# Turning f by DMA transfers in place of TensorE in a fused linear-attention and MLP kernel

## The chip, the core and the metric

The kernel runs on one core of a Trainium2 chip. The metric is device time in microseconds (us), the median of several executions. Times are compared only with runs of the kernel before on the same chip in the same rounds.

Engine names in the profile: PE is TensorE (matrix products and transposes), DVE is VectorE, ACT is ScalarE, POOL is GpSimd, SP is SyncE, which here only issues transfers. "SPq" and "POOLq" are the queues from which SP and GpSimd issue transfers.

## The reference, cut to what matters

```python
# B=4, H=8, S=768, D=48
f = 1 / (1 + exp(-f_logit))
for t in range(S):
    state = f[:, :, t, :, None] * state + einsum('bhd,bhe->bhde', k[:, :, t], v[:, :, t])
    y[:, :, t] = einsum('bhd,bhde->bhe', q[:, :, t], state)
x  = y as (B, S, 384)
xn = (x - mean) / sqrt(var + 1e-6) * g_ln
out = x + maximum(xn @ w_ch1, 0) @ w_ch2          # 384 -> 1536 -> 384
```

Everything is float32. The recurrence is computed in 12 units of 64 tokens, all four batches at once. The weights arrive as 8-byte words and are converted on the chip in the start part.

## The kernel before

The program is written as two lists of tokens, which fix the order of instructions on every engine. `START` holds the first three units with the conversion of the weights. `UNIT` is repeated for the MLP of units 3 to 11 (`m`) with the attention of later units (`n = m+1`, `o = m+2`, `p = m+3`) woven in. `m3` is one step of the MLP of unit 3, `a5.gates` a step of the attention of unit 5, `l6f` the load of unit 6's f.

```python
UNIT = """
m{m} m{m} m{m} a{n}.carried a{o}.after a{n}.scores a{n}.causal m{m} m{m} a{n}.values m{m} m{m}
m{m} m{m} a{n}.stats m{m} m{m} m{m} a{n}.norm m{m} m{m} m{m} s{m} a{n}.chunk
m{m} a{n}.turn m{m} a{o}.upto a{p}.gates a{o}.kx l{p}v a{o}.k a{n}.state m{m} m{m} m{m}
a{o}.kt y{n} m{m} a{o}.q l{p}q l{p}x a{o}.kept l{p}k m{m} l{z}f
"""
```

f comes with tokens in the partitions and is wanted with channels there. TensorE turns it, eight transposes of 128x128, and ScalarE takes the sigmoid out of PSUM. `fraw` is one buffer: the next load waits until it has been read.

```python
def across(src, g):
    pt = one_bank(f"tr{n}")
    for a in range(NP):
        nc.tensor.transpose(pt[:, a * P:(a + 1) * P],
                            src[:, g, 2 * a:2 * a + 2].rearrange("p h e -> p (h e)"), ident)
    return pt.rearrange("p (s t) -> p s t", t=T)

def do_gates():
    ...
    for g in range(G):
        pt = across(loaded[n, "f"], g)
        nc.scalar.activation(out=gv[:, segs, 1:E1], in_=pt, func=AF.Sigmoid)
```

The LayerNorm's `rstd` is made on GpSimd; xn on VectorE needs it. Behind xn in VectorE's order stands an add that is needed by ScalarE's relu, and the fifth of the six matmul steps of p1 reads what that relu writes:

```python
def do_stats():
    ...                                        # mean and variance on VectorE
    nc.gpsimd.tensor_scalar_add(out=rstd, in0=mv[:, :, 1], scalar1=EPS)
    nc.gpsimd.tensor_tensor(out=rstd, in0=rstd, in1=power, op=ALU.pow)

# by_blocks, the first layer:
    add((1, 2), product("bz", y[6], b[2, 2]))  # VectorE, behind xn in its order
    relu((1, 2))                               # ScalarE
# the second layer:
    nc.scalar.copy(out=p1, in_=product("p1", a11, b11))   # steps 5 and 6 read block (1, 2)
```

Of the kernel before, what the change touches and what calls it, by code (L numbers as in the profile page):

```python
# [8 lines left out]
FP32 = mybir.dt.float32  # L9
I32 = mybir.dt.int32  # L10
U32 = mybir.dt.uint32
AF = mybir.ActivationFunctionType
ALU = mybir.AluOpType
PSUM = bass.MemoryType.PSUM
# [288 lines left out]


START = """
l0k f l0q a0.gates l0x a0.after l0v f r a0.kx a0.upto l1f
d a0.kept a0.k d l1x d d a0.q l1k a0.carried d a0.scores
d a0.causal a0.values w d r a0.kt a0.stats f l1q d a1.gates
f l1v a0.chunk d w a0.norm a1.after a0.state a0.turn d a1.upto a1.kx
a1.k d f r w m0 a1.kept m0 a1.q f f r  # L310
w a1.carried a1.kt r f r l2k f a1.scores a1.causal f l2v
w l2f f a1.values r a1.chunk f a1.stats m0 m0 r w
a1.norm m0 a1.turn r w r w a1.state m0 m1 m1 m1
w m1 w a2.gates r m0 m1 m0 a2.after r l2x w
l2q w a2.kx a2.k a2.upto m1 m0 a2.q m0 m0 l3q l3k
a2.kept l3v m0 a2.carried a2.scores U m1 a2.causal a2.values m1 a2.stats a2.norm
m1 m1 U l3f a2.kt U m1 a2.turn m1 a3.gates T a2.chunk
m2 a3.after a2.state a3.kx l3x l4f m2 a3.k a3.upto a3.kept m2 a3.q
U m2 U l4q a3.carried a3.scores a3.kt U U a3.causal U l4x
a4.gates l4k a3.values T l4v U U a3.chunk m2 a3.stats a3.state t  # L320
l5v U a3.norm m2 s2 a4.after m2 l5f a3.turn m2 m2 a4.kx
a4.k a4.upto l5x l5k m2 U u m2 a4.q m2 y3 l5q
a5.gates a4.kt m2 l6f a4.kept
"""
UNIT = """
m{m} m{m} m{m} a{n}.carried a{o}.after a{n}.scores a{n}.causal m{m} m{m} a{n}.values m{m} m{m}
m{m} m{m} a{n}.stats m{m} m{m} m{m} a{n}.norm m{m} m{m} m{m} s{m} a{n}.chunk
m{m} a{n}.turn m{m} a{o}.upto a{p}.gates a{o}.kx l{p}v a{o}.k a{n}.state m{m} m{m} m{m}
a{o}.kt y{n} m{m} a{o}.q l{p}q l{p}x a{o}.kept l{p}k m{m} l{z}f
"""  # L330


# [1 line left out]
def kernel(  # L334
# [19 lines left out]
    nc = tc.nc  # L354
    B, H, S, D = q.shape
    P = 128
    T = 64
    G = B // 2
    NP = H // 2
    GA = G * NP  # L360
    NS = 2 * GA
    E1 = T + 1
# [4 lines left out]
    NU = S // T  # L367
# [2 lines left out]
    LEAST = 1e-12  # L370
    PLAIN = 2
    FIRST = 3
    PIECE = 768

    outer = ctx.enter_context(tc.tile_pool(name="outer", bufs=1))
# [9 lines left out]
    raws = fast.enter_context(tc.tile_pool(name="raws", bufs=2))  # L385
    work = fast.enter_context(tc.tile_pool(name="work", bufs=1))
    xs = fast.enter_context(tc.tile_pool(name="xs", bufs=3))
    ps2 = fast.enter_context(tc.tile_pool(name="ps2", bufs=2, space=PSUM))
    ps1 = fast.enter_context(tc.tile_pool(name="ps1", bufs=4, space=PSUM))

    changing = ExitStack()
    stage = changing.enter_context(tc.tile_pool(name="stage", bufs=2))

    def two_banks(name):
        return ps2.tile([P, 2, 512], FP32, tag="two", name=name)

    def one_bank(name):
        return ps1.tile([P, 512], FP32, tag="one", name=name)
# [11 lines left out]
    def load(n, name, engines=(nc.sync,)):  # L410
        if n >= NU:
            return
        if name == "x":

            loaded[n, name] = raws.tile([P, G, NP, D], FP32, tag="rawx", name=f"vx{n}")
            odd = v.rearrange("b (a r) s d -> b r s a d", r=2)
            for b in range(B):
                nc.sync.dma_start(out=loaded[n, name][(1 - b % 2) * T:(2 - b % 2) * T, b // 2],
                                  in_=odd[b, 1, n * T:(n + 1) * T])
            return  # L420
        if name == "v":
            vt = raws.tile([P, G, H, D], FP32, tag="rawv", name=f"v{n}")
            loaded[n, name] = vt
        else:
            loaded[n, name] = wide_heads[name]
        src = {"f": f_logit, "k": k, "q": q, "v": v}[name]
        for b in range(B):
            engines[b % len(engines)].dma_start(  # L428
                out=loaded[n, name][(b % 2) * T:(b % 2 + 1) * T, b // 2, :, 0:D],
                in_=src[b, :, n * T:(n + 1) * T, :].rearrange("h p d -> p h d"))  # L430

    load(0, "f", (nc.sync, nc.scalar))

# [161 lines left out]
    def attention(n):  # L595
# [7 lines left out]
        def new(name, shape, **kw):  # L603
            at[name] = work.tile(shape, FP32, tag=name, name=f"{name}{n}", **kw)
            return at[name]
# [6 lines that stand above are left out]
                                    src[:, g, 2 * a:2 * a + 2].rearrange("p h e -> p (h e)"),  # L612
                                    ident)
            return pt.rearrange("p (s t) -> p s t", t=T)
# [20 lines left out]
        def times(dst, pts, by):  # L635
            for g, pt in enumerate(pts):
                segs = slice(g * HS, (g + 1) * HS)
                nc.vector.tensor_tensor(out=dst[:, segs], in0=pt, in1=by[:, segs, 1:E1],  # L638
                                        op=ALU.mult)

        def do_gates():
            new("after", [P, NS, E1])
            new("upto", [P, NS, E1])
            new("total", [P, NS], bufs=2)
            for g in range(G):
                segs = slice(g * HS, (g + 1) * HS)
                pt = across(loaded[n, "f"], g)
                nc.scalar.activation(out=gv[:, segs, 1:E1], in_=pt, func=AF.Sigmoid)  # L648
                if n == 0:
                    scan_after(segs)  # L650
                    scan_upto(segs)
# [7 lines left out]
                scan_upto(slice(0, NS))  # L659

        def do_k_across():
            at["pk"] = [across(loaded[n, "k"], g) for g in range(G)]

        def do_k():
            times(new("kh", [P, NS, T]), at["pk"], at["after"])

        def do_q():
            times(new("qh", [P, NS, T]), [across(loaded[n, "q"], g) for g in range(G)],
                  at["upto"])
            nc.vector.tensor_tensor(out=least, in0=least, in1=at["total"], op=ALU.min)  # L670

        def do_kept():
# [6 lines left out]

        def do_carried():  # L680

            at["py"] = py = two_banks(f"py{n}")
            if not n:
                return
            qh, kept = at["qh"], at["kept"]
            for e in range(GA):
                for b in range(2):
                    for r in range(2):
                        nc.tensor.matmul(py[half(b), r, e * D:(e + 1) * D],  # L689
                                         lhsT=qh[head_rows(r), 2 * e + b],  # L690
                                         rhs=kept[head_rows(r), b, e], start=e == 0, stop=False,
                                         skip_group_check=True)
# [285 lines left out]




    running = {}

    def run(plan):
        for token in plan.split():
            kind, rest = token[0], token[1:]
            if kind == "a":
                n, stage = rest.split(".")
                if int(n) >= NU:
                    continue  # L990
                if "a" + n not in running:
                    running["a" + n] = attention(int(n))
                running["a" + n].pop(stage)()
            elif kind == "m":
                if token not in running:
                    running[token] = mlp(int(rest))
                next(running[token])
            elif kind == "l":
                load(int(rest[:-1]), rest[-1])
            elif kind == "s":  # L1000
                sums(int(rest))
            elif kind == "y":
                if FIRST <= int(rest) < NU:
                    sums_of_x(int(rest))
            else:
                {"r": read, "w": write, "f": fetch, "t": mix, "d": idle,
                 "T": lambda: mix(nc.gpsimd), "u": mix_step,
                 "U": lambda: mix_step(nc.gpsimd)}[token]()
# [2 lines left out]
    assert not (queue or fetched or opened)  # L1011
    for m in range(3, NU):
        run(UNIT.format(m=m, n=m + 1, o=m + 2, p=m + 3, z=m + 4))
        if m == NU - 2:
            worst = consts.tile([P, 1], FP32)
            nc.vector.tensor_reduce(out=worst, in_=least, axis=mybir.AxisListType.X, op=ALU.min)
            pw = one_bank("pw")
            nc.tensor.transpose(pw[0:1, 0:P], worst, ident)
            least_one = consts.tile([1, 1], FP32)
            nc.vector.tensor_reduce(out=least_one, in_=pw[0:1, 0:P], axis=mybir.AxisListType.X,  # L1020
                                    op=ALU.min)
            nc.vector.tensor_scalar(out=small, in0=least_one, scalar1=LEAST, scalar2=None,
                                    op0=ALU.is_lt)
# [37 lines left out]
```

## Time and profile before

The kernel before takes 476.49 us (475.71 to 476.61). Its profiled execution was a quicker one, of 472.8 us.

| | before |
|---|---|
| span of the profiled execution | 470.7 us |
| TensorE busy | 96% |
| GpSimd busy | 20% |
| first product of the first repeated unit (bw of m3) | 152.52 us |
| one repeated unit | 36.13 us |

Two more lines are used later. The first is from the page's groups (line, engine, operation, names, shapes, count, then total busy us, mean ns of one, and idle us ahead of the group). The second fence is the windows view of one unit: for each engine busy us and, in brackets, its instructions, then TensorE's granted clock, DMA share and GB/s.

```profile
L935 PE MATMUL pp<-w,h 128*128 128x192 f32 x240 | 42.9, 329 | 0.0
```

```profile
297.03:333.16 36.13, 36.13 (x500) 35.43 (x499) 26.95 (x48) 11.46 (x24) 3.64 (x6) 1.00 0.32 62
```

One instruction takes 329 ns; two of them, which overlap with their neighbours, make one step of a product. TensorE never waits ahead of this group. In the unit it is busy for 36.13 us of 36.13 at full clock, VectorE for 27, GpSimd for 3.6. So TensorE's work is the time, and GpSimd seems free.

### The profile page before, as it was taken

How to read it: one execution, taken by the hardware profiler on the slowest of the kernel's cores; microseconds unless marked ns; L12 is line 12 of the kernel's file. 1: busy time of each engine (PE TensorE's matmuls, PEld its weight loads, DVE VectorE, ACT ScalarE, POOL GpSimd, SP SyncE). 2: the span in 40 equal slices, each digit the busy share in tenths (PEclk: the TensorE clock that was granted, in tenths of full speed). 3: DMA queues.
4: the chain of work that ended last, by engine and by line, in shares of the span. 5: the costliest groups of instructions: out<-in, count | busy, mean ns of one | idle time of the engine just before them, and what ended most of it. 6: DMA issues, size and time to landing. Idle time of an engine off the chain costs nothing.

```text
span 470.7 us, 13070 instructions
## 1 busy us (share of the span) xinstructions
PE 452.5 (96%) x5655; PEld 420.3 (89%) x5655; DVE 332.3 (71%) x543; ACT 149.7 (32%) x298; POOL 93.9 (20%) x110
## 2 busy tenths in 40 slices
PE   5698999999999999999999999999999999999994
PEld 4487887668899999999999999999999999999994
DVE  6798978236698688578678678677768768666361
ACT  3256652013321341341251242243142241241320
POOL 3215534079222011011011011002002002002010
PEclk9989999999999999999999999999999999999998
DMA  9899980623463302512522522422422410100001
GB/s 167 163 215 239 262 218 2 135 45 65 81 117 78 76 3 55 99 35 52 96 43 52 101 37 50 87 54 43 92 54 42 78 36 9 29 1 18 17 10 33
DMA packets 125969, 36.32 MB, mean 77 GB/s; under 512 B 116432, under 2 KB 122064, under 8 KB 125904
## 3 DMA queue, kind: packets, MB, share of 16 engines
q1 hardware_dynamic: 124128, 35.02, 36.3%
q8 instruction: 46, 0.75, 0.7%
q10 hardware_dynamic: 1776, 0.40, 0.4%
q14 instruction: 19, 0.16, 0.1%
HBM read 30.67 MB, written 4.72 MB: 75 GB/s over the span
## 4 chain that ended last, share of the span: by engine, by line
PE 90%; DVE 3%; SPq 3%; DMA 1%; issue 0%; ACT 0%
PE pp L935 29%; PE bx L844 11%; PE ph L906 9%; PE by L844 9%; PE po L916 7%; PE tr L611 6%; PE bz L844 3%; PE py L729 3%; PE py L689 3%; PE ps L703 2%; PE pn L759 2%; PE kp L719 2%; SPq L428 2%; PE bv L844 2%; PE bw L844 2%; PE xp L792 2%
## 5 line engine op out<-in xcount | busy, mean ns | idle before, releaser
L906 PE MATMUL ph<-xt,w 128*128 128x256 f32 x216 | 48.6, 381 | 0.5 <-DVE kh L638 0.5
L906 PEld LDWEIGHTS ph<-xt,w 128*128 128x128 f32 x216 | 40.4, 190 | 6.5 <-issue 0.9
L935 PE MATMUL pp<-w,h 128*128 128x192 f32 x240 | 42.9, 329 | 0.0
L935 PE MATMUL pp<-mixed,h 128*128 128x192 f32 x240 | 42.3, 326 | 0.0
L935 PE MATMUL pp<-mixed,s 128*128 128x192 f32 x240 | 40.9, 326 | 0.0
L855 ACT ACTIVATE h<-h 128x512 f32<-128x512 f32 x45 | 28.3, 630 | 38.5 <-DVE h L852 37.2
L935 PEld LDWEIGHTS pp<-mixed,h 128*128 128x128 f32 x240 | 39.1, 190 | 0.0
L935 PEld LDWEIGHTS pp<-mixed,s 128*128 128x128 f32 x240 | 38.9, 190 | 0.1
L935 PEld LDWEIGHTS pp<-w,h 128*128 128x128 f32 x240 | 38.6, 190 | 0.4
L747 POOL TENSOR_SCALAR rstd<-mv 128x2 f32<-128x2 f32 x12 | 2.8, 235 | 180.8 <-DVE mv L746 180.7
L852 DVE TENSOR_TENSOR h<-h,by 128x512 f32<-128x512 f32 x36 | 24.8, 688 | 16.9 <-PE by L844 15.9
L619 DVE TENSOR_TENSOR_SCAN after<-gates,ends 128x1040 f32<-128x1040 f32 (+1 forms) x13 | 28.8, 2213 | 5.8 <-ACT gates L648 5.8
L916 PE MATMUL po<-w,h 128*128 128x384 f32 x96 | 32.5, 488 | 0.0
L721 ACT COPY kt<-kp 128x512 f32<-128x512 f32 x24 | 12.9, 591 | 57.5 <-PE kp L719 57.5
L707 DVE TENSOR_TENSOR sc<-ps,causal 128x1024 f32<-128x1024 f32 x12 | 14.7, 1225 | 22.9 <-PE ps L703 22.9
L631 DVE TENSOR_TENSOR_SCAN upto<-gates,starts 128x1040 f32<-128x1040 f32 (+1 forms) x13 | 29.7, 2282 | 0.5
L852 DVE TENSOR_TENSOR h<-h,bx 128x512 f32<-128x512 f32 x27 | 18.3, 679 | 15.9 <-PE bx L844 15.9
L844 PE MATMUL bx<-y,v 128*128 128x128 f32 x216 | 29.4, 279 | 0.0
L736 ACT COPY x<-py 128x384 f32<-128x384 f32 x24 | 10.3, 483 | 59.0 <-PE py L729 59.0
L916 PEld LDWEIGHTS po<-w,h 128*128 128x128 f32 x96 | 17.8, 190 | 10.8
L844 PEld LDWEIGHTS bx<-y,v 128*128 128x128 f32 x216 | 26.2, 192 | 0.7
L943 POOL TENSOR_TENSOR p1x<-p,x 128x192 f32<-128x192 f32 x10 | 10.3, 1032 | 70.9 <-ACT p L950 70.9
(153 smaller groups left out, 940.0 us busy)
## 6 DMA issues: line engine op xcount, KB each, us to landing
w_0words<-in_moe_w_ch_dram SPq DMA_DIRECT2D x7, 768.0 KB, 5.6
kraw<-in_k_dram SPq DMA_DIRECT2D x48, 96.0 KB, 3.4
qraw<-in_q_dram SPq DMA_DIRECT2D x48, 96.0 KB, 3.0
v<-in_v_dram SPq DMA_DIRECT2D x48, 96.0 KB, 3.0
fraw<-in_f_logit_dram SPq DMA_DIRECT2D x46, 96.0 KB, 3.0
vx<-in_v_dram SPq DMA_DIRECT2D x48, 48.0 KB, 2.8
out_dram<-p1x SPq DMA_DIRECT2D x19, 48.0 KB, 2.0
out_dram<-u4y SPq DMA_DIRECT2D x19, 48.0 KB, 2.0
```

Of the source, the lines that this page charges most:

```text
L611: nc.tensor.transpose(pt[:, a * P:(a + 1) * P], src[:, g, 2 * a:2 * a + 2].rearrange("p h e -> p (h e)"), ident)
L619: nc.vector.tensor_tensor_scan(out=at["after"].rearrange(flat)[:, c0:c1][:, ::-1], data0=gt[:, c0 + 1:c1 + 1][:, ::-1], data1=ends.rearran ...
L631: nc.vector.tensor_tensor_scan(out=at["upto"].rearrange(flat)[:, c0:c1], data0=gt[:, c0:c1], data1=starts.rearrange(flat)[:, c0:c1], initi ...
L689: nc.tensor.matmul(py[half(b), r, e * D:(e + 1) * D], lhsT=qh[head_rows(r), 2 * e + b], rhs=kept[head_rows(r), b, e], start=e == 0, stop=F ...
L707: nc.vector.tensor_tensor(out=new("sc", [P, 2, GA, T]).rearrange("s r e t -> s (r e) t"), in0=at["ps"].rearrange("s r e t -> s (r e) t"), ...
L729: nc.tensor.matmul(py[half(b), r, e * D:(e + 1) * D], lhsT=sc[rows, r, e], rhs=vx[rows, g, a] if r else vt[rows, g, 2 * a], start=n == 0 a ...
L844: nc.tensor.matmul(banks[bank][:, i], lhsT=right[:, i * P:(i + 1) * P], rhs=left, start=new and i == 0, stop=True, skip_group_check=True)
L852: nc.vector.tensor_tensor(out=out[to], in0=out[to], in1=bank, op=op)
L855: nc.scalar.activation(out=out[to], in_=out[to] if bank is None else bank, func=AF.Relu)
L906: nc.tensor.matmul(ph[:, j], lhsT=w1[:, m, (i + j) * P:(i + j + 1) * P], rhs=xt[:, m], start=m == 0, stop=m == KD - 1)
L916: nc.tensor.matmul(po, lhsT=h[:, i, g * P:(g + 1) * P], rhs=w2[:, i], start=i == 0, stop=i == KF - 1)
L935: nc.tensor.matmul(pp, lhsT=a[:, i], rhs=b[:, i], start=i == 0, stop=i == KH - 1)
```

## The change

The intent is to take f's transposes from TensorE. From unit 4 on (`DIRECT = 4`, counted from 0), GpSimd takes each half of f apart into a plane of low and a plane of high 16-bit halves, sends them to DRAM, and a transposing transfer of two-byte elements from SP's queue brings them back turned and interleaved into floats again. Besides, the state's products (`chunk`) follow the values' directly, the two-bank PSUM pool, one tag with two buffers, becomes two tags with one buffer each (`py` gets its own, scores and state products share the other), a reduction of the final check stands one unit earlier, and the start plan is new. The `START` plan's diff is left out here: it has five dummy matmuls fewer (11 to 6), one weight-mixing step more on GpSimd, and the tokens `p4f x4f` and `p5f x5f`.

```diff
+    turned = dict.fromkeys("f")
+    def split(n, name):
+        ...
+        for g in range(G):
+            planes = raws.tile([P, 2, 64 * H], U16, tag="planes", bufs=1, ...)
+            nc.gpsimd.tensor_copy(
+                out=planes.rearrange("p two c -> p c two"),
+                in_=raw[:, g].rearrange("p h e -> p (h e)").bitcast(U16).rearrange(
+                    "p (c two) -> p c two", two=2))
+            nc.gpsimd.dma_start(out=there[g], in_=planes)
+    def transfer(n, name):
+        ...
+        for g in range(G):
+            nc.sync.dma_start_transpose(out=..., in_=there[g].rearrange("p two c -> (p two) c"))
 ...
+            if is_direct(n, "f"):
+                nc.scalar.activation(out=gv[:, :, 1:E1], in_=turned["f"], func=AF.Sigmoid)
+                return
 ...
-    ps2 = fast.enter_context(tc.tile_pool(name="ps2", bufs=2, space=PSUM))
+    ps2 = fast.enter_context(tc.tile_pool(name="ps2", bufs=1, space=PSUM))
 ...
-            at["py"] = py = two_banks(f"py{n}")
+            at["py"] = py = two_banks(f"py{n}", "out")
```

The new repeated plan; `p{p}f` is the split, `x{p}f` the transposing transfer:

```
m{m} m{m} m{m} a{n}.carried a{n}.scores a{o}.after a{n}.causal m{m} p{p}f m{m} a{n}.values a{n}.chunk
m{m} m{m} m{m} a{n}.stats m{m} x{p}f m{m} m{m} m{m} a{n}.norm m{m} m{m}
m{m} s{m} m{m} a{n}.turn m{m} a{p}.gates a{o}.kx l{p}v a{o}.k m{m} a{o}.upto m{m}
m{m} a{o}.kt y{n} m{m} a{n}.state a{o}.q l{p}q l{p}x l{p}k a{o}.kept m{m} l{z}f
```

`p{p}f` stands ahead of `a{n}.stats`. On GpSimd that puts the split ahead of rstd. `l{z}f`, the load of the f to be split, is still the last in SP's queue.

More of the change, by code (lines that the diff above doesn't have):

```diff
@@ L11 @@
 U32 = mybir.dt.uint32
+U16 = mybir.dt.uint16
 AF = mybir.ActivationFunctionType
@@ L305 @@
 START = """
-l0k f l0q a0.gates l0x a0.after l0v f r a0.kx a0.upto l1f
-d a0.kept a0.k d l1x d d a0.q l1k a0.carried d a0.scores
-d a0.causal a0.values w d r a0.kt a0.stats f l1q d a1.gates
-f l1v a0.chunk d w a0.norm a1.after a0.state a0.turn d a1.upto a1.kx
-a1.k d f r w m0 a1.kept m0 a1.q f f r
-w a1.carried a1.kt r f r l2k f a1.scores a1.causal f l2v
-w l2f f a1.values r a1.chunk f a1.stats m0 m0 r w
-a1.norm m0 a1.turn r w r w a1.state m0 m1 m1 m1
-w m1 w a2.gates r m0 m1 m0 a2.after r l2x w
@@ L315 @@
-l2q w a2.kx a2.k a2.upto m1 m0 a2.q m0 m0 l3q l3k
-a2.kept l3v m0 a2.carried a2.scores U m1 a2.causal a2.values m1 a2.stats a2.norm
-m1 m1 U l3f a2.kt U m1 a2.turn m1 a3.gates T a2.chunk
-m2 a3.after a2.state a3.kx l3x l4f m2 a3.k a3.upto a3.kept m2 a3.q
-U m2 U l4q a3.carried a3.scores a3.kt U U a3.causal U l4x
-a4.gates l4k a3.values T l4v U U a3.chunk m2 a3.stats a3.state t
-l5v U a3.norm m2 s2 a4.after m2 l5f a3.turn m2 m2 a4.kx
-a4.k a4.upto l5x l5k m2 U u m2 a4.q m2 y3 l5q
-a5.gates a4.kt m2 l6f a4.kept
+l0k f l0q a0.gates a0.after l0x l0v r f a0.kx a0.upto l1f
@@ new lines @@
+d a0.k d l1k a0.kept l1x d a0.q a0.carried f a0.scores a0.causal
+a0.values w f r l1q a0.stats l1v a0.kt w a1.gates f a0.chunk
+a0.norm a0.turn f a1.after a0.state a1.upto a1.kx r m0 a1.kept d w
+a1.k m0 r a1.q w f d a1.carried a1.scores f l2k a1.causal
+a1.kt d r l2v f a1.values r r f m0 a1.chunk l2f
+f m0 l2x w a1.stats w m0 a1.norm a1.turn r w m0
+r m1 r f l2q a1.state m1 m1 w m1 a2.gates m1
+w w a2.after r w a2.kx r w a2.k a2.upto m1 m0
+l3k m0 m0 a2.q l3q a2.kept l3v m0 m0 m0 l3f a2.carried
@@ L324 @@
+a2.scores U m1 a2.causal a2.values m1 U l3x a2.stats a2.norm m1 a2.kt
+m1 U m1 m1 T a2.turn a3.gates a2.chunk m2 a2.state a3.after l4f
+p4f x4f a3.kx a3.k a3.upto a3.kept U m2 a3.q m2 m2 a3.carried
+U l4q a3.scores U a3.causal U a3.kt a4.gates a3.values U U U
+U l4k T l4v a4.after T a3.chunk m2 a3.stats a3.state a3.norm l5v
+m2 s2 l5f p5f x5f m2 a4.kx l5k m2 m2 a4.k a4.upto
+m2 l4x U a5.gates a4.q m2 a3.turn l5x l5q m2 u y3
+a4.kept m2 a4.kt l6f
 """
 UNIT = """
-m{m} m{m} m{m} a{n}.carried a{o}.after a{n}.scores a{n}.causal m{m} m{m} a{n}.values m{m} m{m}
@@ L327 @@
-m{m} m{m} a{n}.stats m{m} m{m} m{m} a{n}.norm m{m} m{m} m{m} s{m} a{n}.chunk
-m{m} a{n}.turn m{m} a{o}.upto a{p}.gates a{o}.kx l{p}v a{o}.k a{n}.state m{m} m{m} m{m}
-a{o}.kt y{n} m{m} a{o}.q l{p}q l{p}x a{o}.kept l{p}k m{m} l{z}f
+m{m} m{m} m{m} a{n}.carried a{n}.scores a{o}.after a{n}.causal m{m} p{p}f m{m} a{n}.values a{n}.chunk
+m{m} m{m} m{m} a{n}.stats m{m} x{p}f m{m} m{m} m{m} a{n}.norm m{m} m{m}
+m{m} s{m} m{m} a{n}.turn m{m} a{p}.gates a{o}.kx l{p}v a{o}.k m{m} a{o}.upto m{m}
+m{m} a{o}.kt y{n} m{m} a{n}.state a{o}.q l{p}q l{p}x l{p}k a{o}.kept m{m} l{z}f
@@ L372 @@
     FIRST = 3
+    DIRECT = 4
     PIECE = 768
@@ L392, with two_banks @@
     stage = changing.enter_context(tc.tile_pool(name="stage", bufs=2))
-    def two_banks(name):
-        return ps2.tile([P, 2, 512], FP32, tag="two", name=name)
+    def two_banks(name, tag="two"):
+        return ps2.tile([P, 2, 512], FP32, tag=tag, name=name)
     def one_bank(name):
@@ L430, in load, with is_direct @@
                 in_=src[b, :, n * T:(n + 1) * T, :].rearrange("h p d -> p h d"))
+    turned = dict.fromkeys("f")
+    drams = fast.enter_context(tc.tile_pool(name="drams", bufs=1, space=bass.MemoryType.DRAM))
+    halved = {}
+    def is_direct(n, name):
+        return n >= DIRECT and name in turned
+    def split(n, name):
+        if n >= NU or not is_direct(n, name):
+            return
+        raw = wide_heads[name]
+        there = drams.tile([G, P, 2, 64 * H], U16, tag=f"{name}halves{n % 2}", name=f"{name}halves{n}")
+        halved[n, name] = there
+        for g in range(G):
+            planes = raws.tile([P, 2, 64 * H], U16, tag="planes", bufs=1, name=f"{name}planes{n}_{g}")
+            nc.gpsimd.tensor_copy(
[4 more added lines that the diff above has]
+    def transfer(n, name):
+        if n >= NU or not is_direct(n, name):
+            return
+        if not turned[name]:
+            turned[name] = late["pool"].tile([P, NS, T], FP32, name=f"{name}turned")
+        there = halved.pop((n, name))
+        for g in range(G):
+            to = turned[name].rearrange("p (g s) t -> p g (s t)", g=G)[:, g].bitcast(U16)
+            nc.sync.dma_start_transpose(
+                out=to.rearrange("p (a r) -> p a r", a=NP),
+                in_=there[g].rearrange("p two c -> (p two) c"))
     load(0, "f", (nc.sync, nc.scalar))
@@ L644, in do_gates @@
             new("total", [P, NS], bufs=2)
+            if is_direct(n, "f"):
+                nc.scalar.activation(out=gv[:, :, 1:E1], in_=turned["f"], func=AF.Sigmoid)
+                return
             for g in range(G):
@@ L661, in do_k_across @@
         def do_k_across():
-            at["pk"] = [across(loaded[n, "k"], g) for g in range(G)]
+            if not is_direct(n, "k"):
+                at["pk"] = [across(loaded[n, "k"], g) for g in range(G)]
         def do_k():
-            times(new("kh", [P, NS, T]), at["pk"], at["after"])
-        def do_q():
-            times(new("qh", [P, NS, T]), [across(loaded[n, "q"], g) for g in range(G)],
-                  at["upto"])
+            kh = new("kh", [P, NS, T])
+            if is_direct(n, "k"):
+                nc.vector.tensor_tensor(out=kh, in0=turned["k"], in1=at["after"][:, :, 1:E1],
+                                        op=ALU.mult)
+            else:
+                times(kh, at["pk"], at["after"])
+        def do_q():
+            qh = new("qh", [P, NS, T])
+            if is_direct(n, "q"):
+                nc.vector.tensor_tensor(out=qh, in0=turned["q"], in1=at["upto"][:, :, 1:E1],
+                                        op=ALU.mult)
+            else:
+                times(qh, [across(loaded[n, "q"], g) for g in range(G)], at["upto"])
             nc.vector.tensor_tensor(out=least, in0=least, in1=at["total"], op=ALU.min)
@@ L999, in run @@
                 load(int(rest[:-1]), rest[-1])
+            elif kind in "px":
+                {"p": split, "x": transfer}[kind](int(rest[:-1]), rest[-1])
             elif kind == "s":
@@ L1013 @@
         run(UNIT.format(m=m, n=m + 1, o=m + 2, p=m + 3, z=m + 4))
-        if m == NU - 2:
+        if m == NU - 3:
             worst = consts.tile([P, 1], FP32)
             nc.vector.tensor_reduce(out=worst, in_=least, axis=mybir.AxisListType.X, op=ALU.min)
+        if m == NU - 2:
             pw = one_bank("pw")
```

## The prediction

> **What bounds the kernel now.** I read the page first (busy shares, slices), then the chain of waits, then the order of time on each engine in one repeating unit of 64 tokens, then the start-up.
>
> ```profile
> PE 452.5 (96%) x5655; PEld 420.3 (89%) x5655; DVE 332.3 (71%) x543; ACT 149.7 (32%) x298; POOL 93.9 (20%) x110
> PE   5698999999999999999999999999999999999994
> POOL 3215534079222011011011011002002002002010
> ```
>
> TensorE is busy in all slices but the first four and the last. The chain agrees: 90% of it is PE. GpSimd (POOL) has much room, except in slices 9 and 10, about 94 to 118 us, where it prepares mixed weights.
>
> From about 44 us to the end each microsecond taken from TensorE's stream counts, and each wait put into it is lost. The time of a unit is the distance of two equal pieces of the chain:
>
> ```profile
> 299.87 1.08 PE py L689 x64
> 336.00 1.08 PE py L689 x64
> ```
>
> 336.00 - 299.87 = 36.13 us. All of it is work: the windows view of 297.9 to 334.0 gives PE 36.10 of 36.10 us. DVE has 26.91 of 36.1, POOL 3.64. The pieces that the change touches, in order of time:
>
> ```profile
> 312.29 1.06 PE L844 MATMUL bx<-y,v 128*128 128x128 f32 x8
> 313.18 1.06 PE L844 MATMUL by<-y,v 128*128 128x128 f32 x8
> 314.17 1.15 PE L759 MATMUL pn<-v,kt 64*64 64x48 f32 x64
> 315.25 2.22 PE L935 MATMUL pp<-w,h 128*128 128x192 f32 x12
> 319.91 1.04 PE L611 MATMUL tr<-ident,fraw 128*128 128x128 f32 x8
> 320.78 1.04 PE L611 MATMUL tr<-ident,kraw 128*128 128x128 f32 x8
> ```
>
> Durations overlap, so I use the distance of the starts: f's eight transposes hold TensorE for 320.78 - 319.91 = 0.87 us, and a state product (pn) standing alone for 1.08.
>
> **What the Trainium skill says.** "TensorE: Matmul & The Clock Gate", Part 4, gives about 275 ns for a transpose in a kernel's context; this trace has a median of 273. But the gain is the pitch, 0.87 / 8 = 0.11 us each. "DMA: Bandwidth & Descriptors", Anatomy of one DMA (GpSimd's path), gives 2.0 us plus bytes / 436e3 us: an estimate of 2.6 us for one half of the planes (262,144 bytes). No transfer of GpSimd is in this trace; the 48 KB stores from SP land in 2.0. "GPSIMD Engine Reference", 3.1, gives at best 1.03 to 1.8 cycles an element at 1.2 GHz: 0.9 to 1.5 us for a copy of 1024, as an estimate 1.3. Here a fill of 1041 elements took about 0.93. "VectorE: DVE Perf Modes", The three transpose paths, gives 1309 ns for 128x128 of two bytes through the DMA crossbar: eight such blocks in a half would be 10.5 us if nothing overlapped. I take 4 as an estimate; no run shows it.
>
> **What the change saves.** (1) Units 4 to 11 lose eight transposes each. Six of these sets are in the repeated plan, two in the start-up plan: 8 x 0.87 = 7.0 us. (2) The state's products follow the values' directly, in seven repeated units. A lone group of 64x64 products costs 1.08 us and makes the next piece 0.20 longer (bx 1.09 against 0.89, pp 2.15 against 1.95); where pn follows py directly (128.39 in the chain) it costs 0.93. So 0.15 + 0.20 = 0.35 us, 7 x 0.35 = 2.5. The separate PSUM tags make this possible; I see no wait they remove, as TensorE has none. (3) The final check's reduction comes earlier: about 0.5. Sum: 10 us, 2.1%. Everything had to be hidden for this, and I do not think it is.
>
> **What it adds, in a repeated unit.** GpSimd's order in the changed program is: copy half 0, send it; copy half 1, send it; then the two small operations that make rstd. The second copy waits for the first send, since there is one planes buffer. I count from the unit's first product (bw, 297.03 = 333.16 - 36.13, and 333.16). What it collides with:
>
> ```profile
> 311.11 0.22 POOL L747 TENSOR_SCALAR rstd<-mv 128x2 f32<-128x2 f32 x1 [19.41 <-DVE mv L746]
> 312.32 0.87 DVE L782 TENSOR_SCALAR xn<-x,mv,rstd 128x384 f32<-128x384 f32 x2
> 313.10 0.68 DVE L852 TENSOR_TENSOR h<-h,bz 128x512 f32<-128x512 f32 x1
> 313.81 0.63 ACT L855 ACTIVATE h<-h 128x512 f32<-128x512 f32 x1 [0.75 <-DVE h L852]
> 341.98 3.32 SPq L428 DMA_DIRECT2D fraw<-in_f_logit_dram  x4
> ```
>
> The load of f stands last in SP's queue: it starts at +8.8 (341.98 - 333.16). I take it about 0.9 later after the change, as the out store before q's load will wait longer for DVE. Two issues of 0.65 us, and 3.0 to landing: half 0 is there at about +13.2. Before, TensorE wanted it only at +22.9 and the lateness cost nothing; now the split wants it at once. Then copy 1.3, send 2.8 with its issue, copy 1.3, issue 0.3, rstd 1.0: rstd is done at about +20.0, where it used to be at about +15. Behind rstd on DVE are xn (0.87), the add of bz (0.70), then ACT's relu (0.63) and some 0.15 of hand-over: +22.35. In both programs the fifth of p1's six products waits for that relu. Without the delay p1 starts at +18.05 (pn is no longer ahead of it) and needs the relu four products of 0.325 later, at +19.35. So TensorE waits 22.35 - 19.35 = 3.0 us. The unit becomes 36.13 - 0.87 - 0.35 + 3.0 = 37.9, or 1.8 longer. It happens where an f is split, in six units: 6 x 1.8 = +11 us. With the shortest copies and send the wait is 1.5 and the six units cost +2; with slow ones it is 5 and they cost +23.
>
> The crossbar transfers themselves should be hidden: half 1 starts at about +21.5, and ACT needs f only before the copies of kt at about +32. At 10 us each, one after the other, they would not be.
>
> **What it adds in the start-up.** In the old kernel GpSimd mixes weights from 97.6 to 121, without a gap. In the new order the split of f4 stands in the middle of that work, f4's load must wait for f3's transposes (one raw buffer), and a third mixing step moves from DVE to GpSimd. From the end of f3's transposes, in us: load 4.7; copy, send, copy, issue 5.9; eight mixing operations at 1.35, 10.8; eight more (two sets of four at about 4.2 a set), 8.4; rstd 1.0; xn 0.9; two sums on DVE 1.9. Sum 33.6. TensorE reaches the product that needs the second sum after 28.6 of work (92.0 - 63.4 in my tally of the new order by the pitches above). That is a wait of 5. Then the split of f5 also stands before p1x on GpSimd, and p1x frees a bank that p5 needs: some 3 more. The order near 33 us puts a weight conversion (2 us on DVE) ahead of kh: 0 to 2 more. Against this stand f5's 0.87 and five fewer dummy matmuls, mostly in time that is idle anyway. So the repeated part starts 7 to 9 us later than at 152.5; I take 8.
>
> Sum: 476.5 + 11 (six units, their f and pn savings inside) + 8 (start-up) - 0.5 (check) - 0.4 (the seventh pn) = 494.6. Since I have stacked waits where some may overlap, and since a plan retuned for this change may fit better than I can see, I pull it to 491.
>
> **Rivals.** (a) All is hidden: 466 to 468, faster by about 2%. For it: GpSimd is 80% free, and the new order moves the split early. Against it: early in GpSimd's order is no help while the load of f lands at +13. (b) The crossbar transfer is the bound: 10 us or more a half puts ACT's sigmoid past the copies of kt, 4 to 7 us a unit, 500 to 515. Against it: some 15 us of room between the first send and kt. (c) Only rstd waits, and briefly (load earlier, short copies), with a mild start-up: gains and losses cancel, 475 to 482. (d) GpSimd's reads slow DVE's two-input operations (the scans, about 2.4 us each): a few tenths a unit.
>
> **Range and chances.** Rival (c) gives the lower end, slow copies and sends with the start-up wait the upper: 478 to 506. The limit of slower by 2% is 486. Faster 0.11, within 2% 0.29, slower 0.60.
>
> **What would show it.** Right: p1 split in two in TensorE's order of time, with 2 to 4 us before its fifth product; the wait of xn on DVE for rstd; rstd at +19 or later, behind the second copy; a wait of several us near 140 us before the product of mixed weights and s. Wrong: units of 34.9 us with no idle TensorE; the split over before +14; or ACT waiting for the turned f, which would be rival (b).

## The result, and the profile after

The changed kernel is correct and takes 574.52 us (573.5 to 577.87, four runs), beside 476.19 us for the kernel before in the same rounds. The ratio is 1.208 (95% interval 1.203 to 1.213). 491 us was predicted, with 478 to 506 as the range; the direction was right and the size far off.

The page after: busy shares, slices (each digit a fortieth of the span), the shares of the chain of waits that ended last, and three groups.

```profile
PE 467.5 (82%) x5581; PEld 431.5 (75%) x5581; DVE 342.7 (60%) x539; ACT 147.9 (26%) x290; POOL 184.1 (32%) x146
...
PE   5789999998249949938975991994699299999995
...
POOL 2324441449971351081053125206213510101101
PEclk9689999999758969987996997998699699999999
...
PE 52%; POOL 19%; SPq 12%; DMA 11%; issue 2%; DVE 2%; ACT 1%; ACTq 0%; POOLq 0%
...
L453 POOL COPY fplanes<-fraw 128x1024 uint16<-128x1024 uint16 x16 | 76.4, 4774 | 139.9 <-DMA fraw<-in_f_logit_dram 125.3
L988 PE MATMUL pp<-w,h 128*128 128x192 f32 x240 | 53.1, 376 | 63.5 <-ACT h L908 63.5
...
L835 DVE TENSOR_SCALAR xn<-x,mv,rstd 128x384 f32<-128x384 f32 x24 | 19.4, 848 | 81.2 <-POOL rstd L801 81.2
```

The row of PE now has a hole in every unit, and a deep one at slices 11 and 12. PE's share of the chain has gone from 90% to 52%; GpSimd and transfers have come into it. The group that was free of waits (pp<-w,h, which is p1 and p2) now has 63.5 us of idle TensorE ahead of it, which ends with ScalarE's relu. xn has 81.2 us of idle VectorE ahead of it, which ends with GpSimd's rstd. And one copy of the split takes 4774 ns. PEclk shows that TensorE's granted clock was lower in many slices.

One unit in order of time (start, duration, engine, line, operation, count; in brackets idle time ahead and what ended it). The unit begins with bw at 325.17.

```profile
339.73 4.77 POOL L453 COPY fplanes<-fraw 128x1024 uint16<-128x1024 uint16 x1 [19.17 <-DMA fraw<-in_f_logit_dram]
344.80 0.63 POOL L457 DMA_DIRECT2D fhalves<-fplanes  x1 [0.30 <-POOL fplanes L453]
347.24 4.69 POOL L453 COPY fplanes<-fraw 128x1024 uint16<-128x1024 uint16 x1 [1.82 <-DMA fhalves<-fplanes]
...
353.15 0.73 POOL L801 TENSOR_TENSOR rstd<-rstd,power 128x2 f32<-128x2 f32 x1
...
353.91 0.87 DVE L835 TENSOR_SCALAR xn<-x,mv,rstd 128x384 f32<-128x384 f32 x2 [12.56 <-POOL rstd L801]
354.69 0.68 DVE L905 TENSOR_TENSOR h<-h,bz 128x512 f32<-128x512 f32 x1
...
355.41 0.63 ACT L908 ACTIVATE h<-h 128x512 f32<-128x512 f32 x1 [13.39 <-DVE h L905]
...
343.15 1.47 PE L988 MATMUL pp<-w,h 128*128 128x192 f32 x8
356.09 1.65 PE L988 MATMUL pp<-w,h 128*128 128x192 f32 x4 [11.48 <-ACT h L908]
357.53 1.49 PE L845 MATMUL xp<-ident,xn 128*128 128x128 f32 x6
```

This is the predicted chain link by link: load, copy, send, copy, rstd, xn, add of bz, relu, fifth step of p1. But TensorE waits 11.48 us where 3.0 were predicted. The transposes of xn after the wait take 1.49 us, where the same six take 0.82 in the kernel before. The granted clock in the 3.3 us after the wait was 0.50.

Where the 101.3 us of longer span (572.0 against 470.7) lie follows from the times of bw, the first product of a unit:

| | bw of m3 | bw of m9 | six units between | rest |
|---|---|---|---|---|
| before | 152.52 | 369.53 | 217.0 | 101.2 |
| after | 182.67 | 472.17 | 289.5 | 99.8 |
| difference | +30.2 | | +72.5 | -1.4 |

One unit became 48.2 us long, the start 30.2 us longer. (By the medians of the timed executions the loss is 98 us; the profiled execution of the kernel before was a quick one. The first 100 us, before any split, also vary: the third unit's rstd on GpSimd began at 95.9 to 102.2 us in single executions of one and the same start plan. So differences of whole starts are sure to a few us only.)

### The profile page after: what moved, and what is told of

It is laid out like the page before. It is cut to its first block, busy times and chain, and to the rows that moved or that the text cites. A ratio compares the mean times of both kernels' runs of the same rounds, so it can differ in the third digit from the quotient of the medians.

```text
span 572.0 us, 13005 instructions
## 1 busy us (share of the span) xinstructions
PE 467.5 (82%) x5581; PEld 431.5 (75%) x5581; DVE 342.7 (60%) x539; ACT 147.9 (26%) x290; POOL 184.1 (32%) x146
## 4 chain that ended last, share of the span: by engine, by line
PE 52%; POOL 19%; SPq 12%; DMA 11%; issue 2%; DVE 2%; ACT 1%; ACTq 0%; POOLq 0%
PE pp L988 24%; POOL fplanes L453 13%; SPq L430 7%; DMA fraw<-in_f_logit_dram 6%; PE po L969 5%; PE ph L959 5%; PE tr L651 3%; DMA fhalves<-fplanes 3%; PE bx L897 3%; SPq L420 3%; PE by L897 2%; POOL v L612 2%; PE xp L845 2%; SPq L1001 2%; PE kp L772 2%
## 5 line engine op out<-in xcount | busy, mean ns | idle before, releaser
L453 POOL COPY fplanes<-fraw 128x1024 uint16<-128x1024 uint16 x16 | 76.4, 4774 | 139.9 <-DMA fraw<-in_f_logit_dram 125.3
L988 PE MATMUL pp<-w,h 128*128 128x192 f32 x240 | 53.1, 376 | 63.5 <-ACT h L908 63.5
L988 PEld LDWEIGHTS pp<-w,h 128*128 128x128 f32 x240 | 47.2, 226 | 65.3 <-ACT h L908 65.2
L835 DVE TENSOR_SCALAR xn<-x,mv,rstd 128x384 f32<-128x384 f32 x24 | 19.4, 848 | 81.2 <-POOL rstd L801 81.2
L988 PE MATMUL pp<-mixed,s 128*128 128x192 f32 x240 | 45.0, 347 | 17.7 <-DVE s L877 14.7
L988 PEld LDWEIGHTS pp<-mixed,s 128*128 128x128 f32 x240 | 42.4, 204 | 18.5 <-issue 15.0
L996 POOL TENSOR_TENSOR p1x<-p,x 128x192 f32<-128x192 f32 x10 | 12.2, 1225 | 59.8 <-ACT p L1003 59.8
L789 ACT COPY x<-py 128x384 f32<-128x384 f32 x24 | 10.3, 481 | 64.8 <-PE py L782 64.8
```

The costliest lines, as they stand in the source:

```text
L453: nc.gpsimd.tensor_copy(out=planes.rearrange("p two c -> p c two"), in_=raw[:, g].rearrange("p h e -> p (h e)").bitcast(U16).rearrange("p ...
L835: nc.vector.tensor_scalar(out=xn[:, g], in0=x[:, g], scalar1=mv[:, g, 0:1], scalar2=rstd[:, g:g + 1], op0=ALU.subtract, op1=ALU.mult)
L988: nc.tensor.matmul(pp, lhsT=a[:, i], rhs=b[:, i], start=i == 0, stop=i == KH - 1)
```

## The experiments

Theory A: the split stands ahead of rstd in GpSimd's order, begins only when a late load lands, and its slow copies set the wait. Rival B: the transposing transfers are the cost. Rival C: the new plan and the single PSUM buffers are. Rival D: GpSimd's copies slow VectorE by sharing its way into SBUF. A further question (E) was whether the lower clock is a result of the waits.

### plan_only: no f by transfers, all else as changed

```diff
-    DIRECT = 4
+    DIRECT = 99
```

> Every f on TensorE again; the new plan and the PSUM tags stay. Theory A (GpSimd's split ahead of rstd makes both the longer unit and most of the longer start): the unit falls from 48.8 to 35.6 to 36.2 us, p1 is not cut in two, and the kernel takes 476 to 492 us, the uncertain part being the new start plan. Theory C (the new plan and the single PSUM buffers are what costs): it stays above 540 us.

Measured: 476.76 us, ratio 1.008 (1.004 to 1.012). Units of 36.0 us, bw of m3 at 158.78. C falls as the main cause: plan and tags together move the time by less than 1%.

### no_crossbar: split and sends, but f turned on TensorE

```diff
-            if is_direct(n, "f"):
-                nc.scalar.activation(out=gv[:, :, 1:E1], in_=turned["f"], func=AF.Sigmoid)
-                return
 ...
-            nc.sync.dma_start_transpose(...)
```

> Split and sends as in the changed kernel, but no transposing transfer: f is turned on TensorE as before. Theory A: the wait before p1's fifth product stays 11 to 12 us, TensorE has 7 us more work, 572 to 588 us. Theory B (the transposing transfers, or what they do to other transfers, are the cost): the wait goes, below 520 us.

Measured: 584.02 us. TensorE's wait before p1's fifth step is up to 12.6 us (64.8 us over six units), and the eight transposes are back. B falls: without a single transposing transfer the loss is as large. In the changed kernel these transfers land 3.3 us after their issue and ScalarE waits for them twice in the start (32 us at the longest) and never in a repeated unit. The start does not hang on those two either: without the transfers bw of m3 is at 183.2, as late as with them (182.7).

### plain_copy: as no_crossbar, the same bytes copied straight

```diff
-                out=planes.rearrange("p two c -> p c two"),
-                in_=raw[:, g].rearrange("p h e -> p (h e)").bitcast(U16).rearrange(
-                    "p (c two) -> p c two", two=2))
+                out=planes.rearrange("p two c -> p (two c)"),
+                in_=raw[:, g].rearrange("p h e -> p (h e)").bitcast(U16))
```

(The planes are not read afterwards, so the result stays right.)

> As no_crossbar, with the same 1024 16-bit elements copied straight, without taking them apart. If the price of the copy is in the pattern, it falls from 4.7 to 1.0 to 1.5 us, the wait in the unit from 11.5 to about 4 to 5 us, and the kernel takes 520 to 540 us. If it is in the number of elements, or in DVE's use of SBUF at the same time, it stays at 4.7 us and the time is that of no_crossbar.

Measured: 521.12 us; a copy takes 1037 ns in the median, not 4741. So 1024 elements of 16 bits are not slow on GpSimd. The pattern is.

### split_order: the two loops of the split exchanged

```diff
-                out=planes.rearrange("p two c -> p c two"),
+                out=planes,
 ...
-                    "p (c two) -> p c two", two=2))
+                    "p (c two) -> p two c", two=2))
```

> The changed kernel with the loops of the split exchanged: writes go on in sequence, reads step by 4 bytes. If the alternating writes were the cost, the copy falls to 1.5 to 2.5 us and the kernel to 525 to 550 us; if reads and writes count alike, or elements do, it stays near 4.7 us and 570 to 578 us.

Measured: 517.85 us, ratio 1.094 (1.089 to 1.099), lower than I had expected even for the good case. The same elements come to the same places, only the order differs. The group:

```profile
L453 POOL COPY fplanes<-fraw 128x1024 uint16<-128x1024 uint16 x16 | 17.5, 1093 | 143.0 <-DMA fraw<-in_f_logit_dram 127.5 <-DMA fhalves<-fplanes 15.5
```

1093 ns on average in place of 4774. In this order reads that step by 4 bytes cost nothing over the straight copy (both have a median of 1037 ns). With writes that alternate between two planes 1024 bytes apart, the copy took 4.6 times as long. That order also makes the innermost rows of the written pattern two elements long, where they are 512 after the exchange; no run separates the short rows from the distance of the writes. By the profiled executions the order is worth 17.6 us of the start (bw of m3 at 165.09; 16.8 if counted from the third unit's rstd) and 41.5 us of the six units (248.0 in place of 289.5), 59 of the 101 us; by the ratios (1.208 and 1.094) it is 54 of the 98.

A unit of this kernel, which begins at 204.76, is the unit that I had predicted, with a copy of 1.0 in place of 1.3 us:

```profile
220.47 1.03 POOL L453 COPY fplanes<-fraw 128x1024 uint16<-128x1024 uint16 x1 [20.32 <-DMA fraw<-in_f_logit_dram]
...
226.48 0.73 POOL L801 TENSOR_TENSOR rstd<-rstd,power 128x2 f32<-128x2 f32 x1
...
222.74 1.47 PE L988 MATMUL pp<-w,h 128*128 128x192 f32 x8
229.43 1.65 PE L988 MATMUL pp<-w,h 128*128 128x192 f32 x4 [5.22 <-ACT h L908]
```

p1 starts at +17.98 (predicted 18.05). The load is there at +15.7, not +13.2, and rstd is ready at +22.4, not +20.0. The wait is 5.2 us, not 3.0.

### fill: matmuls of zeros in the gap

```diff
+                if name == "p1" and i == 4 and n <= NU - DIRECT:
+                    for _ in range(25):
+                        nc.tensor.matmul(bank[:, 256:512], lhsT=nothing,
+                                         rhs=nothing..., start=False, stop=False, ...)
```

> The changed kernel with 25 matmuls of zeros put into TensorE's stream before p1's fifth product in the six units that split an f: 25 x 0.43 = 10.8 us of work that nobody reads, where TensorE waits 11.5 us. If the slower products after the wait (1.49 us for xn's transposes in place of 0.82) come from the idle time itself, they return to 0.8 and the unit falls from 48.8 to 46 to 47 us, the kernel to 556 to 566 us. If the lower clock has another reason, the time stays at 574 or rises.

Measured: 567.16 and 567.23 us, ratio 1.197, 1.2 us over the upper end that I gave. Two units of it in order of time:

```profile
304.65 0.92 PE L994 MATMUL pp<-w,h 128*128 128x192 f32 x4
305.40 0.82 PE L845 MATMUL xp<-ident,xn 128*128 128x128 f32 x6
306.06 2.12 PE L994 MATMUL pp<-w,h 128*128 128x192 f32 x12
...
352.99 0.92 PE L994 MATMUL pp<-w,h 128*128 128x192 f32 x4 [2.38 <-ACT h L908]
353.75 0.95 PE L845 MATMUL xp<-ident,xn 128*128 128x128 f32 x6
354.49 3.70 PE L994 MATMUL pp<-w,h 128*128 128x192 f32 x12
```

In the first, the zeros fill the gap, and everything after it has its normal length. In the second a gap of 2.38 us is left, the granted clock is 0.50 from 354.3 to 357.7, and p2 takes 3.70 us in place of 2.12. In a third unit a gap of 1.86 us (until 402.51) was followed by full clock. So the lower clock follows from the waits, as E says; it adds to them and is no cause of its own. The units are 47.2 us long on average, 1.1 shorter than the changed kernel's, though TensorE had 11 us more to do in each.

### early_load: the slow split as it is, its load earlier in SP's queue

```diff
-m{m} m{m} m{m} a{n}.stats m{m} x{p}f m{m} ...
+m{m} m{m} m{m} a{n}.stats m{m} x{p}f l{z}f m{m} ...
 ...
-... a{o}.kept m{m} l{z}f
+... a{o}.kept m{m}
```

> The changed kernel, slow copies and all, with one token moved: the load of the next f right behind the transposing transfers in SP's queue, not at its end. Theory A (the order split, then rstd, with a load that lands too late): the split is over at +12 us of the unit, rstd no longer waits, p1 is whole from the second repeated unit on, units of 34.9 to 36.5 us, and the kernel takes 500 to 520 us; the start stays long. Theory D (copies on GpSimd slow VectorE by their reads of SBUF, wherever they stand): units stay above 40 us and the kernel above 535.

Measured: 535.78 us, ratio 1.131. Theory A is half right here. The wait of xn for rstd is gone from the second repeated unit on. But the units became 40.0 to 43.1 us long (40.3 and 40.5 for those of m4 and m5), not 35 to 36.5, and the total is what D had named. Why is on VectorE and GpSimd in order of time:

```profile
262.74 4.76 POOL L453 COPY fplanes<-fraw 128x1024 uint16<-128x1024 uint16 x1
...
270.22 4.72 POOL L453 COPY fplanes<-fraw 128x1024 uint16<-128x1024 uint16 x1 [1.81 <-DMA fhalves<-fplanes]
...
263.09 4.36 DVE L867 TENSOR_TENSOR y<-xt 128x256 f32<-128x256 f32 x2
...
271.50 2.85 DVE L723 TENSOR_TENSOR least<-least,total 128x16 f32<-128x16 f32 x1
```

The same two operations in order_early, the next run, which differs in the order of the copy's loops alone:

```profile
237.89 0.16 DVE L723 TENSOR_TENSOR least<-least,total 128x16 f32<-128x16 f32 x1
...
267.47 1.29 DVE L867 TENSOR_TENSOR y<-xt 128x256 f32<-128x256 f32 x2
```

The two sums y began 0.35 us after GpSimd's copy; the first of them took 4.03 us, until 0.4 us before the copy's end at 267.50, and the second its usual 0.41. `least`, 16 elements a partition, began 1.3 us into the next copy and took 2.85 us in place of 0.16. Together they lose 5.8 us a unit, and the unit is 5.3 longer than with short copies (40.3 against 35.0). TensorE's waits show it too: over five units it waits 10.0 us for u4x and 5.6 us for `kept`, which stand behind these operations on VectorE. The Trainium skill states this in "SBUF — State Buffer", Who interferes with whom: a VectorE instruction with two inputs in SBUF contends with a GpSimd instruction that reads SBUF, and the one that comes first blocks the other. This trace agrees, but for the 0.4 to 0.6 us by which the blocked operations ended before the copies' recorded ends; and VectorE's products qh in the same copy, which read one input from PSUM, kept their usual 0.68 us. In the changed kernel the copies fell into VectorE's own wait for rstd, so the effect was hidden there behind the larger one. It is not why the copies are slow: they last 4.7 us in both places.

### order_early: both, loops exchanged and load early

The diffs of split_order and early_load together.

> Loops of the split exchanged and the load early. Theory A: units of 34.9 us, the saved transposes show; the start still has late splits ahead of rstd3: 478 to 492 us. If the start of split_order (m3's first product at about 169 us, 17 later than before) is the plan's own and not the copies', the upper end.

Measured: 480.4 us, ratio 1.013 (1.010 to 1.017). The first repeated unit, whose load still comes late, takes 41.1 us; the following take 34.9 to 36.3. The saving is there as soon as split and rstd do not collide. The start (bw of m3 at 160.84) keeps the kernel above the one before.

### old_start_plan_only and old_start_order_early: the start plan of before

`START` is that of the kernel before. In the first every f stays on TensorE (`DIRECT = 99`); in the second, which also has the changes of order_early, f goes by transfers from the seventh unit on (`DIRECT = 6`).

> The start plan of the kernel before, every f on TensorE, with the new repeated plan and the PSUM tags. If plan_only's late first unit (158.8 us against 152.5) belongs to the new start plan, it begins at 152 to 155 us here and the kernel takes 470 to 474 us; the repeated plan's own gain is then the rest, 0.1 to 0.35 us a unit. If the single PSUM buffers cost the time at the start, it begins near 158 again.

> As order_early with the start plan of the kernel before, f direct from the seventh unit on (the first split is in the first repeated unit). Theory A: start as before at 152.5 us, first repeated unit 2 to 5 us long by its late load, then units of 34.9 us: 466 to 475 us, ratio 0.98 to 1.00. Above 480 us the transfers collide with something that I have not seen.

Measured: old_start_plan_only 472.53 us, ratio 0.995 (0.993 to 0.997); old_start_order_early 470.28 us, ratio 0.992 (0.988 to 0.996). The first has the time that I expected, though not the trace: its profiled execution was the slowest of five (476.35 us) and begins m3 at 157.3, so I take the start plan's price from the ratios: 1.0078 - 0.9949 = 1.3%, about 6 us. The two ratios are from different chips, each against the kernel before on its own. Whether the single PSUM buffers cost something at the start stays open: in all five traces with the old start plan and the new tags, bw of m3 comes at 154.1 to 157.3, against 152.52 in the one trace of the kernel before.

old_start_order_early beats both kernels.

> The best version so far once more, in five rounds: 0.988 to 0.996 of the kernel before.

Measured: 467.56 us, ratio 0.986 (0.983 to 0.988), a little better than expected. In the same rounds old_start_plan_only has 0.995, so the transfers of f are worth 0.9%, about 4.4 us, and the rearranged unit and PSUM tags 0.5%, about 2.4 us. A unit of it:

```profile
254.91 1.03 POOL L453 COPY fplanes<-fraw 128x1024 uint16<-128x1024 uint16 x1
...
258.68 1.03 POOL L453 COPY fplanes<-fraw 128x1024 uint16<-128x1024 uint16 x1 [1.81 <-DMA fhalves<-fplanes]
...
237.68 0.22 POOL L800 TENSOR_SCALAR rstd<-mv 128x2 f32<-128x2 f32 x1 [12.08 <-DVE mv L799]
...
242.65 2.12 PE L988 MATMUL pp<-w,h 128*128 128x192 f32 x12
```

The copies of the next split run at the end of the unit without a wait for the load; rstd waits only for its own input, mv; p1 is one piece of twelve matmuls again.

### k_too and k_q_too: k, and k and q, by transfers too

```diff
-    turned = dict.fromkeys("f")
+    turned = dict.fromkeys("fk")            # k_q_too: "fkq"
 ...  (kh's and qh's own tiles take the transfer; k_q_too also has p{o}q behind a{n}.norm and x{o}q ahead of a{o}.kt)
-... m{m} p{p}f m{m} a{n}.values a{n}.chunk
+... m{m} p{p}f p{o}k m{m} a{n}.values a{n}.chunk
-... x{p}f l{z}f m{m} ...
+... x{p}f l{z}f x{o}k m{m} ...
```

> As old_start_order_early, and from the seventh unit on k goes the same way as f, turned into kh's own tile and multiplied there. Six units lose another 0.87 us of TensorE: about 5 us less than old_start_order_early, 463 to 468 us, if GpSimd's four copies and sends (about 13 us, from the end of one unit to +10 us of the next) stay ahead of rstd at +13 us. If they do not, xn waits for rstd again and the time is 470 us or more.

> k and q both by transfers, q's split behind rstd. If nothing else binds, another 5 us less, 458 to 464 us. Against it: VectorE has 27 of 35 us busy and stands while GpSimd copies, so its sums for the next unit's products may come late: then 465 to 480 us, with TensorE waiting for u4x, y or qh.

Measured: 481.49 us, ratio 1.014 (1.007 to 1.020, so it is unclear whether it is slower by 2%), and 490.23 us, ratio 1.035. The gain came in neither. k_too is what the second branch of its expectation said, 470 us or more with xn waiting for rstd; k_q_too lies above both ranges. (One of its four executions, 493.48 us, is the slow one; the mean of the other three is 1.029 of the kernel before.) k_too walked into the trap of the original change. I had moved f's load and left k's, so k's copy waits for its load, and rstd stands behind it:

```profile
316.08 1.04 POOL L453 COPY kplanes<-kraw 128x1024 uint16<-128x1024 uint16 x1 [10.89 <-DMA kraw<-in_k_dram]
...
322.74 0.22 POOL L804 TENSOR_SCALAR rstd<-mv 128x2 f32<-128x2 f32 x1
...
323.81 0.87 DVE L839 TENSOR_SCALAR xn<-x,mv,rstd 128x384 f32<-128x384 f32 x2 [3.47 <-POOL rstd L805]
```

mv was ready at about 317.1; rstd began at 322.74. TensorE waits 10.3 us before p1's fifth steps over the six units, which are 13.5 us longer than in old_start_order_early_again though k's transposes are gone; what else they lose I have not taken apart. For k_q_too the trace shows TensorE waiting 8.3 us for `kept` and 4.8 us for a later sum of VectorE; how these arise I have not taken apart, and whether k and q could pay with earlier loads stays open.

## Why the prediction was wrong

**Right in mechanism.** The predicted signs are all there, though not in their size: p1 in two pieces (with 11.48 us between them, not 2 to 4), xn waiting for rstd, rstd behind the second copy, a wait before the product of mixed weights and s in the start (14.7 us). Its rivals (a) and (b) fell, (b) by no_crossbar. Its saving per set of transposes was close: 6 x 0.87 = 5.2 us against 4.4 by the ratios for the six units of the best version, whose units take 34.9 to 35.2 us in place of 36.0. The saving of the rearranged unit, 2.5 us, is met by 2.4, though by the ratios and not shown to be the cause named: the unit itself fell by 0.1 to 0.2 us, not 0.35.

**The term that failed: "copy 1.3, send 2.8 with its issue, copy 1.3".** The two copies took 4.77 and 4.69 us, 6.9 more for both. From the end of the first to the start of the second it took 2.7, as assumed. I took a duration per element from the skill's page and did not ask how this copy walks: two elements at a time, each to another plane. split_order shows that this was it. With the loops exchanged the copy took 1.04 us, less than the 1.3 assumed, and the kernel 1.094 times the time before in place of 1.208. The upper end of the range, "slow copies and sends", allowed for the wait to be 5 us; the copies were slower than any case I had considered.

**A second term of the same sum: the load's landing.** "Half 0 is there at about +13.2" was +14.5 in the changed kernel and +15.7 in split_order, where its issue began at +10.7. That accounts for 2.5 us, and so for the wait of 5.2 in place of 3.0 there. Part of it was a slip: the terms as they stand, 8.8 + 0.9 + 2 x 0.65 + 3.0, make +14.0. And the same prediction allowed 4.7 us for this load in the start, but from +9.7 to +13.2 only 3.5 here; in the changed kernel it took 4.8 (issue at +9.7). Together: 3.0 + 6.9 + 1.3 (load) = 11.2, against 11.48 measured.

**A term that was missing.** The sum treats a wait as its own length. After it TensorE ran at a lower clock; fill shows that it is a result of the wait. The unit shown is 48.3 us long (325.17 to 373.45); less 11.48 of wait, 36.8 are left, where plan_only's 36.0 less the 0.87 for f's transposes make 35.1. So about 1.7 us went to the lower clock, which fits the granted clock of 0.50 for 3.3 us after the wait; fill recovered 1.1 on average.

**The start: 30.2 us later, not 8.** Here again the copies are the larger part. From the third unit's rstd, which precedes every split, to bw of m3 it takes 81.0 us in the changed kernel, 64.2 in split_order, 65.0 in order_early, 56.7 in plan_only and 55.9 in the kernel before. So the slow copies cost 16 to 17 us, and the split with quick copies 7.4 to 8.2. That this is near the 5 + 3 of the prediction is partly luck: in split_order the wait before the product of mixed weights and s is 6.8 us, where I had 5, the clock is lowered behind it, and there is no wait for p1x, where I had 3 (it is there with the slow copies, 3.0 us in the changed kernel). The new start plan by itself costs about 6 us by the ratios (plan_only against old_start_plan_only), where I allowed 0 to 2; after that rstd it costs only 0.8, and before it single executions vary by as much, so its place is not shown.

**Rival (d)** was given "a few tenths a unit". In the changed kernel it is hidden, but early_load shows that a long GpSimd copy in a busy stretch of VectorE costs 5.8 us a unit. The estimate was right only for short copies.

The pull from 494.6 to 491, for waits that might overlap, went the wrong way.

## What to carry to other kernels

Before work is moved to an engine that is free on the average, ask two things of that engine's order: what stands behind the new work, and when its input lands. Here two tiny operations stood behind it and were due at once. And ask how each operand is walked: exchanging two loops of a copy, with the same elements in the same places, was worth more than half of the whole loss here. With the loops, one load and the start plan put right, the version with transfers is 0.8% to 1.4% faster than the kernel before.

## What the Trainium skill lacked or had wrong

- "GPSIMD Engine Reference", 3.1 and the pitfalls of its section 7, gives costs per element and a penalty for reads with long steps, but no figure for writes that alternate between distant places ("SBUF — State Buffer", Door 1, says only in general that an access which crosses to a new 16-byte line pays a penalty; whether that is what cost the time, no run shows). Here a 16-bit copy of 1024 elements a partition took 1.04 us with writes in sequence, with reads stepping by 4 bytes or not, and 4.74 us with writes alternating between two planes 1024 bytes apart.
- "VectorE: DVE Perf Modes", The three transpose paths, gives 1309 ns for one 128x128 block of two-byte elements through the DMA and a share of the DMA bandwidth for the path, but no time for several blocks. A transposing transfer of 256 KB, eight such blocks, landed in 3.3 us from its issue.
- "TensorE: Matmul & The Clock Gate", the table of "Why this matters for your kernels", warns of gaps over about 3 us. Shorter ones were enough here: in fill a gap of 2.38 us was followed by a granted clock of 0.50 and a product of 3.70 us in place of 2.12; in k_q_too the clock fell to 0.50 after four of six gaps of 1.7 to 1.9 us. A gap of 1.86 us in fill lowered nothing.
